# Two mixture layers after a dynamic convolution on one core: matmuls of 64 rows in both row halves of the array

## Chip, core and metric

The kernel runs on one core of a Trainium2 chip. The metric is the device time of one execution in microseconds; three runs of the kernel before took 1215.25 to 1215.58 us, with a median of 1215.5 us.

## What is computed

A softmax over 7 taps weights a causal convolution of x (2 x 4096 tokens, 192 channels in 8 heads). The result, 8192 tokens of 192 channels, goes through two layers, each a product to 2048 channels, an activation, and a product back to 192:

```python
x = attn_out.reshape(B * S, D)                       # 8192 x 192
h = x @ w_in; g = where(h >= 1, h, where(h <= -1, 0, (h + 1) ** 2 / 4)); x = g @ w_out
h = x @ w_in2; g = h - tanh(h);                                          out = g @ w_out2
```

Each product is made from a high and a low part of both operands, so that its precision is near that of float32: high x high, low x high and high x low. Low x low isn't needed.

## The kernel before

The tokens are cut into 16 blocks `b` of 512. A **stream** `(m, b)` is layer `m` (0 or 1) on block `b`; from block 3 on the streams alternate, (0, b) and then (1, b - 1). A stream has 16 **items** `(m, b, f)`, one for every 128 of the 2048 channels. An item is:

- the first product, `mm1` (L626 to L630): five matmuls of 128 rows x 128 columns with 512 tokens streamed, into one of the PSUM banks 6, 7, 0, 1. The 192 channels of x are one tile of 128 rows for high (`xt[:, 0]`), one for low (`xt[:, 1]`), and one that holds the other 64 channels, high in its upper 64 rows and low in the lower 64 (`xt[:, 2]`). The weights of the last 64 channels stand twice, once per 64 rows. So the fifth matmul, low weights x `xt[:, 2]`, spends 64 of its rows on low x low.
- the activation: for layer 0 on ScalarE twice (L636, L637) and VectorE (L638), for layer 1 on ScalarE (L640) and VectorE (L641); then the high part `gh` on ScalarE (L642) and the low part `gl` on VectorE (L646).
- the second product, `mm2a` and `mm2b` (L654 to L656, L660, L661): five matmuls onto two banks per stream (2 and 3 for layer 0, 4 and 5 for layer 1), which are added up over the 16 items. It comes three items later (`LAG`).

`finish1` (L682 on) turns the two banks of layer 0 into the next layer's x; `finish2` (L701 on) stores those of layer 1. `conv` makes the convolution of a block on VectorE; from block 4 on (`MOVED`) its result is transposed by VectorE in squares of 32 and by way of HBM (`move_rows`, the buffers `spot`), and not on TensorE.

The order of the work on each engine is fixed by a planner, `Plan.run`: each task has a key (the item's number in the order of items, plus an offset), a duration, what it depends on and which buffers it takes, and each engine starts the ready task with the lowest key. VectorE fills its gaps with the convolution of later blocks as far as buffers allow. Within an engine the instructions then run in that order; semaphores order them between engines. Matmuls have no semaphores among themselves, since TensorE runs them one after the other. GpSimd works only in the first items (up to item 56).

Of the kernel before, what the change touches and what calls it, by code (L numbers as in the profile page):

```python
# [157 lines left out]
def on(engine, dur):  # L158
    return {engine: (dur, 0.0)}
# [3 lines left out]
def tile_dynconv_moe_moe(  # L163
# [71 lines left out]
    def bits(w):  # L235
# [119 lines left out]


    xdone = {}
    a_of, b_of = {}, {}

    def conv(b, banks, base, gap):  # L360
        early = b < EARLY
# [186 lines left out]
    def move_rows(b, wg, xw, mem, xt, dep, key):  # L548


        Q = P // 32
        hi_sb = prod_sb.bitcast(F32R)

        area = lambda n: xws[xw.n].rearrange("p j d -> p (j d)")[:, n * T * D:(n + 1) * T * D]

        def squares(e, n, src):
            e.transpose(
                area(n).rearrange("p (c j n) -> p j c n", c=D // 32, j=T),
                src.rearrange("p j (c n) -> p j c n", n=32),
            )  # L560
# [8 lines left out]
        spot = slot("spot")  # L569

        def away(e, n):
            if n == 0:
                spots[spot.n] = dram.tile([2, D, N], F32, tag=f"spot{spot.n}", name=f"spot{b}")
            for q in range(Q):
                to = spots[spot.n][n].rearrange("(c k) t -> k c t", k=32)[:, :, q * P:(q + 1) * P]
                e.dma_start(to, area(n)[q * 32:(q + 1) * 32].rearrange("p (c k) -> p c k", c=D // 32))

        def back(e, n, k):
            if n == 0 and k == 0:
                xt_tile(xt, f"a_{b}")  # L580
            xt_, d = xt_t[xt.n].bitcast(F32), spots[spot.n][n]
            if k == 0:
                e.dma_start(xt_[:, n, :], d[0:P])
            else:
                e.dma_start(xt_[n * D1:(n + 1) * D1, 2, :], d[P:D])

        d0 = plan.add(on("DMA", 2.6), last, lambda e: away(e, 0), [tq], takes=[spot], uses=[xw], late=4.0)
        d1 = plan.add(on("DMA", 2.6), last, lambda e: away(e, 1), [tr, d0], uses=[xw, spot], late=4.0)
        moves = []
        for n, k in ((0, 0), (0, 1), (1, 0), (1, 1)):  # L590
            first = [] if moves else [marks["fin1", b - 1]]
            moves.append(plan.add(
                on("DMA", 1.0), last, lambda e, n=n, k=k: back(e, n, k), [d1 if n else d0] + moves[:1] + first,
                takes=[] if moves else [xt], uses=[spot] + ([xt] if moves else []), late=3.0,
            ))
        xdone[0, b] = moves

# [14 lines left out]
        return (2, 3) if b == 0 else (4, 5)  # L612

    prev1, prev2 = [None], {}

    def item(m, b, f, after):
        i = at[m, b, f]
# [7 lines left out]

        def mm1(e):  # L626
            w, xt = win[m], xt_t[xs.n]
            ops = [(0, 0), (2, 0), (0, 1), (1, 2), (3, 2)]
            for n, (k, c) in enumerate(ops):
                e.matmul(ps[h.n], w[:, k, fs], xt[:, c], start=n == 0, stop=n == len(ops) - 1)  # L630

        first = plan.add(on("PE", 1.135), i, mm1, after + xdone[m, b] + [wdone.get((0, m, f // 2))], takes=[h], uses=[xs], late=0.35)
# [15 lines left out]
        w = wout[m][:, f, :]  # L648
        a, z = f == 0, f == NF - 1
        need = [wdone.get((1, m, f // 2)), prev2.get((m, b))]  # L650
        if m == 0 or b < NB - 1:
# [12 lines left out]
            t = plan.add(on("PE", 0.454), i + LAG + 0.5, mm2b, [t, tlo], uses=[gl] + acc, late=0.35)  # L664
        else:
            def mm2(e):
                q = banks()
                for n in range(T):
                    ts = slice(n * P, (n + 1) * P)
                    if not z:  # L670
                        e.matmul(q[n][:, 0:2 * D], GH()[:, ts], w, start=a, stop=False)  # L671
                    e.matmul(q[n][:, P:P + D], GL()[:, ts], w[:, P:P + D], start=False, stop=False)
                    if z:
                        e.matmul(q[n][:, 0:2 * D], GH()[:, ts], w, start=False, stop=True)

            t = plan.add(on("PE", 1.14), i + LAG + 0.5, mm2, [thi, tlo] + need, takes=acc if a else [], uses=[gh, gl] + ([] if a else acc), late=0.35)
# [5 lines left out]
    def finish1(b, acc, key, t):  # L682
        s, tm = slot("xt"), slot("val")
        b_of[b] = s
        X, M = lambda k: xt_t[s.n][:, k], lambda: vals[tm.n][0:D1]
        p0, p1 = lambda: ps[acc[0].n], lambda: ps[acc[1].n]

        def hi(e):
            xt_tile(s, f"b_{b}")
            e.copy(X(0), p0())  # L690

        h0 = plan.add(on("ACT", 0.60), key, hi, [t], takes=[s], uses=acc)
        h1 = plan.add(on("ACT", 0.60), key, lambda e: e.copy(M(), p1()[D1:P]), [t], takes=[tm], uses=acc)
# [5 lines left out]
        xdone[1, b] = [h0, l0, rh, rl]  # L699

    def finish2(b, acc, key, t):  # L701

        s, tm = slot("raw"), slot("val")
        R = lambda: raws[s.n].rearrange("p a b -> p (a b)").bitcast(F32)
        M = lambda: vals[tm.n][0:D1]
        p0, p1 = lambda: ps[acc[0].n], lambda: ps[acc[1].n]
# [14 lines left out]
            plan.add(on("DMA", 2.6), key, lambda e, c=c: store(e, c), [t0 if c < P // 32 else t1], uses=[s], late=3.0)  # L721

    def finish_last(b, acc, key, t):
        s = slot("raw")
# [21 lines left out]
    for m in range(2):  # L746
        for c in range(NF // 2):
            for kind in range(2):
                weights(kind, m, c, LEAD[m])
    after = {}  # L750
# [60 lines left out]
```

## Time and profile before

| | |
|---|---|
| median of 3 runs | 1215.5 us (1215.25 to 1215.58) |
| the profiled execution, its span | 1214.0 us; its own time beyond the span isn't listed apart |
| TensorE busy | 1177.7 us, 97%, 5192 matmuls |
| TensorE weight loads busy | 967.7 us, 80%, beside the matmuls |
| VectorE busy | 995.7 us, 82% |
| ScalarE busy | 838.7 us, 69% |
| GpSimd busy | 98.7 us, 8%, all in the first 200 us |
| DMA | 58.4 MB, mean 48 GB/s |

The busy time of an engine is the union of its instructions' spans. A matmul's record, 0.39 us here, is longer than the distance to the next matmul, since matmuls overlap. The profile calls the engines PE (TensorE; PEld are its weight loads, LDWEIGHTS), DVE (VectorE), ACT (ScalarE), POOL (GpSimd) and SP (the queue that issues DMAs).

### The profile page before, as it was taken

To read this page: it belongs to the slowest core of one execution; us is meant where nothing else is said; L and a number is where in the kernel's file an instruction comes from. 1 tells how busy PE (TensorE), PEld (TensorE's weight loads), DVE (VectorE), ACT (ScalarE), POOL (GpSimd) and SP (SyncE) were. 2 spreads that over 40 slices of the span, in tenths; PEclk is the share of its full clock that TensorE was granted. 3 is DMA by queue.
4 is the path that set the end of the run, shared out by engine and by line. 5 is a ranking of instruction groups with operands and counts; after the bars stand their busy time and mean duration, and the time that the engine had idled before them with its cause. 6 is when DMAs were issued, how large, how long until landed. Compare 5 with 4: busy or idle time off the path is not lost.

```text
span 1214.0 us, 15286 instructions
## 1 busy us (share of the span) xinstructions
PE 1177.7 (97%) x5192; PEld 967.7 (80%) x5192; DVE 995.7 (82%) x1519; ACT 838.7 (69%) x1499; POOL 98.7 (8%) x85
## 2 busy tenths in 40 slices
PE   3899999999999999999999999999999999999998
PEld 2678778888887888888888888888888888888887
DVE  8999998999999999797987969688666666666665
ACT  4989896775757667586675857667576665757653
POOL 4643650000000000000000000000000000000000
PEclk9999999999999999999999999999999999999999
DMA  7422130231231203030030302102020100100000
GB/s 209 148 69 77 52 117 10 53 103 50 72 89 18 60 30 101 1 73 29 11 92 1 102 1 45 54 5 61 1 66 1 19 22 2 39 1 14 1 8 19
DMA packets 92038, 58.40 MB, mean 48 GB/s; under 512 B 55868, under 2 KB 81082, under 8 KB 91960
## 3 DMA queue, kind: packets, MB, share of 16 engines
q1 hardware_dynamic: 91772, 57.05, 17.2%
q8 instruction: 40, 0.66, 0.2%
q10 hardware_dynamic: 188, 0.39, 0.1%
q14 instruction: 38, 0.31, 0.1%
HBM read 41.67 MB, written 15.73 MB: 47 GB/s over the span
## 4 chain that ended last, share of the span: by engine, by line
PE 88%; DVE 5%; ACT 3%; issue 1%; POOL 1%; DMA 1%; SPq 0%; DVEq 0%; ACTq 0%; POOLq 0%
PE ps L630 44%; PE ps L660 9%; PE ps L661 9%; PE ps L654 9%; PE ps L656 8%; PE ps L655 8%; PE ps L671 1%; DVE prod L426 1%; DVE gl L646 1%; DVE g L638 1%; ACT gh L642 1%; ACT g L636 1%; ACT raw L312 0%; DMA wg<-in_weight_gen_dram 0%; DVE acc L473 0%
## 5 line engine op out<-in xcount | busy, mean ns | idle before, releaser
L642 ACT CAST gh<-g 128x512 fp32r<-128x512 f32 x512 | 315.4, 618 | 215.2 <-DVE g L641 175.0
L646 DVE TENSOR_TENSOR gl<-g,gh 128x512 fp32r<-128x512 f32 x474 | 326.8, 692 | 150.9 <-ACT gh L642 148.7
L630 PE MATMUL ps<-a,win 128*128 128x512 f32 x1280 | 335.7, 393 | 5.9 <-POOL win L341 2.8
L630 PE MATMUL ps<-b,win 128*128 128x512 f32 x1280 | 332.4, 390 | 2.3 <-DVE val L321 2.3
L630 PEld LDWEIGHTS ps<-a,win 128*128 128x128 f32 x1280 | 241.6, 189 | 61.6 <-POOL win L341 4.0
L630 PEld LDWEIGHTS ps<-b,win 128*128 128x128 f32 x1280 | 239.1, 188 | 52.5 <-DVE val L321 3.5
L641 DVE TENSOR_TENSOR g<-ps,g 128x512 f32<-128x512 f32 x256 | 175.2, 686 | 28.8 <-ACT g L640 28.7
L660 PE MATMUL ps<-gl,wout 128*128 128x512 f32 x496 | 194.6, 392 | 1.9 <-DVE gl L646 1.3
L654 PE MATMUL ps<-gh,wout 128*128 128x512 f32 x496 | 194.1, 391 | 2.1 <-ACT gh L642 2.0
L636 ACT ACTIVATE g<-ps 128x512 f32<-128x512 f32 x256 | 152.0, 594 | 63.3 <-PE ps L630 57.2
L661 PE MATMUL ps<-gl,wout 128*128 128x512 f32 x496 | 193.5, 390 | 0.0
L655 PE MATMUL ps<-gh,wout 128*128 128x512 f32 x496 | 193.3, 390 | 0.0
L656 PE MATMUL ps<-gh,wout 128*128 128x512 f32 x496 | 193.2, 390 | 0.0
L640 ACT ACTIVATE g<-ps 128x512 f32<-128x512 f32 x256 | 152.1, 596 | 46.4 <-PE ps L630 45.3
L638 DVE SCALAR_TENSOR_TENSOR g<-ps,g 128x512 f32<-128x512 f32 x256 | 173.1, 680 | 10.6 <-ACT g L637 9.5
L637 ACT ACTIVATE g<-g 128x512 f32<-128x512 f32 x256 | 162.1, 633 | 4.0
L660 PEld LDWEIGHTS ps<-gl,wout 128*128 128x128 f32 x496 | 93.3, 188 | 25.4 <-DVE gl L646 4.5
L654 PEld LDWEIGHTS ps<-gh,wout 128*128 128x128 f32 x496 | 93.2, 188 | 23.6 <-ACT gh L642 4.4
L656 PEld LDWEIGHTS ps<-gh,wout 128*128 128x128 f32 x496 | 93.3, 188 | 19.5
L655 PEld LDWEIGHTS ps<-gh,wout 128*128 128x128 f32 x496 | 93.2, 188 | 19.1
L661 PEld LDWEIGHTS ps<-gl,wout 128*128 128x128 f32 x496 | 93.4, 188 | 18.9
L426 DVE TENSOR_TENSOR prod<-xw,wg 128x768 f32<-128x768 f32 x84 | 82.7, 985 | 0.1
(78 smaller groups left out, 594.6 us busy)
## 6 DMA issues: line engine op xcount, KB each, us to landing
xw<-in_x_dram SPq DMA_DIRECT2D x14, 960.0 KB, 4.8
spot<-xw SPq DMA_DIRECT2D x96, 96.0 KB, 2.4
raw<-in_moe_w_out_dram SPq DMA_DIRECT2D x16, 384.0 KB, 3.2
a<-spot SPq DMA_DIRECT2D x24, 256.0 KB, 3.9
out_dram<-raw SPq DMA_DIRECT2D x360, 16.0 KB, 1.5
raw<-in_moe_w_in_dram SPq DMA_DIRECT2D x16, 256.0 KB, 3.1
raw<-in_moe_w_in_dram SPq DMA_DIRECT2D x32, 128.0 KB, 3.3
a<-spot SPq DMA_DIRECT2D x24, 128.0 KB, 3.7
```

The costliest lines, as they stand in the source:

```text
L630: e.matmul(ps[h.n], w[:, k, fs], xt[:, c], start=n == 0, stop=n == len(ops) - 1)
L636: t = plan.add(on("ACT", 0.60), i, lambda e: e.activation(G_(), H_(), AF.Relu, bias=0.5, scale=0.5), [first], takes=[g], uses=[h], late=0.1)
L637: t = plan.add(on("ACT", 0.537), i, lambda e: e.activation(G_(), G_(), AF.Square), [t], uses=[g])
L638: t = plan.add(on("DVE", 0.605), i, lambda e: e.scalar_tensor_tensor(G_(), H_(), 1.0, G_(), op0=ALU.max, op1=ALU.min), [t], uses=[g, h])
L641: t = plan.add(on("DVE", 0.605), i, lambda e: e.tensor_tensor(G_(), H_(), G_(), op=ALU.subtract), [t], uses=[g, h])
L642: thi = plan.add(on("ACT", 0.527), i, lambda e: e.copy(GH(), G_()), [t], takes=[gh], uses=[g])
L646: tlo = plan.add(engines, i, lambda e: e.tensor_tensor(GL(), G_(), GH().bitcast(F32), op=ALU.subtract), [thi], takes=[gl], uses=[g], lock= ...
L654: e.matmul(p0, w[:, P:2 * P], GH(), start=a, stop=False)
L655: e.matmul(p0, w[:, 0:P], GH(), start=False, stop=False)
L656: e.matmul(p1, w[:, 2 * P:], GH(), start=a, stop=False)
L660: e.matmul(p1, w[:, 2 * P:], GL(), start=False, stop=z)
L661: e.matmul(p0, w[:, P:2 * P], GL(), start=False, stop=z)
```

## The change

In 24 of the 32 streams, (0, 4) to (0, 15) and (1, 3) to (1, 14), no matmul has 128 rows. Each is made by halves, one on rows 0 to 63 of the array (lane 0) and one on rows 64 to 127 (lane 1), with the matching rows of weights and tokens. The fifth matmul of the first product needs one half alone. Two items are taken together (`both`): 18 halves of first products and 20 of second products, issued as 19 steps with one half of each lane (`weave`).

The two lanes are never on the same bank at once. Steps 0 to 8 (`one`): lane 0 has the first products of both items, while lane 1 has its half of the second products of two earlier items. Steps 9 to 13 (`two`) and 14 to 18 (`three`): lane 0 has its half of two second products and lane 1 its half of the two first products. Where a lane takes a bank over, its matmul waits for the other lane's last matmul on it: `relay` puts an empty instruction on GpSimd that waits for that matmul, and `behind` makes the later matmul wait for the relay. The marks are `a`, `b`, `p` and `q`; `b` goes from lane 1's matmul of step 9 to lane 0's of step 12, `p` from lane 0's of step 16 to lane 1's of step 0 of the next block, that is step 19.

For the halves of the fifth matmul in lane 1, the high part of the last 64 channels is needed in rows 64 to 127 too: a tile `x3` in the place of raw buffers 2 and 3, filled by one more DMA per block of layer 0 and one more ScalarE copy per block of layer 1, 12 each. `finish2` stages its output in the raw buffers 0 and 1 alone. After (1, 14) `close` runs the last ten halves of lane 1 by themselves, and (1, 15) runs as before.

```diff
+    def paired(m, b):
+        return b >= MOVED - m and (m, b) != (1, NB - 1)
...
+    HALVES = [slice(0, D1), slice(D1, P)]
...
+    def relay(q):
+        r = nc.gpsimd.nop(nofuse=True)
+        tc.add_manual_dep(r.ins, q.ins.name, SYNC)
+        return r
+
+    def behind(q, r):
+        if r is not None:
+            tc.add_manual_dep(q.ins, r.ins.name, SYNC)
...
+    def chunks(lane, m, b, f, h, xs):
+        rs, fs = HALVES[lane], slice(f * P, (f + 1) * P)
+        ops = [(0, 0), (2, 0), (0, 1), (1, 2)] + ([(3, 2 + lane)] if f % 2 == lane else [])
+        def mm(e, n, k, c):
+            x = x3(x3_of[m, b]) if c == 3 else xt_t[xs.n][rs, c]
+            return e.matmul(ps[h.n], win[m][rs, k, fs], x, start=lane == 0 and n == 0, stop=lane == 1 and n == len(ops) - 1)
...
+    def weave(e, low, high, waits, marks_at):
+        for n in range(max(len(low), len(high))):
+            for lane, ops in ((0, low), (1, high)):
+                if n < len(ops):
+                    q = ops[n](e)
+                    behind(q, fence.get(waits.get((lane, n))))
+                    if (lane, n) in marks_at:
+                        fence[marks_at[lane, n]] = relay(q)
...
+    def both(m, b, f, h0, h1, need):
+        i = at[m, b, f]
+        g0, g1, o0, o1 = i - 3, i - 2, i - 5, i - 4
...
+        def one(e):
+            low = chunks(0, m, b, f, h0, xs) + chunks(0, m, b, f + 1, h1, xs)
+            high = (old_p() + old_q())[:9]
+            weave(e, low, high, {(1, 0): "p", (1, 6): "q"}, {(1, 5): "a"} if have else {(0, 5): "a", (0, 8): "b"})
+        def two(e):
+            low = second(0, 0, g0, P_KINDS) + second(0, 1, g0, Q_KINDS)
+            high = old_q()[3:] + chunks(1, m, b, f, h0, xs)
+            n = len(high) - 4
+            weave(e, low, high, {(0, 0): "a", (0, 3): "b", (1, n): "a"}, {(1, 0): "b"} if n else {})
+        def three(e):
+            low = second(0, 0, g1, P_KINDS) + second(0, 1, g1, Q_KINDS)
+            high = chunks(1, m, b, f + 1, h1, xs)
+            weave(e, low, high, {(1, 0): "b"}, {(0, 2): "p", (0, 4): "q"})
...
+        if paired(1, b):
+            s3 = x3_of[1, b] = slot("x3")
+            xdone[1, b].append(plan.add(on("ACT", 0.525), key, lambda e: e.copy(x3(s3), M()), [r] + x3_free, takes=[s3], uses=[tm]))
...
-        s, tm = slot("raw"), slot("val")
+        s, tm = slot("raw", out_raws), slot("val")
...
+            if (m, b, f) == (1, NB - 2, NF - 1):
+                close(at[m, b, f] + 1)
```

How the change orders TensorE's work: before, in a stream of layer 0, an item's first product (`win0`, into a bank such as `ps7`) is followed by the second product of the item three before it (`wout0`, onto banks 2 and 3, which are one tile `ps2`); `x5` are five matmuls in a row.

```order
L630 MATMUL ps7_68<-a_9_4924,win0_81 128x512 x5
L654 MATMUL ps2_63<-gh0_98,wout0_83 128x512 [waits Activation_49]
L655 MATMUL ps2_63<-gh0_98,wout0_83 128x512
L656 MATMUL ps2_63<-gh0_98,wout0_83 128x512
L660 MATMUL ps2_63<-gl2_104,wout0_83 128x512 [waits DVE_49]
L661 MATMUL ps2_63<-gl2_104,wout0_83 128x512
L630 MATMUL ps0_65<-a_9_4924,win0_81 128x512 x5
```

In the change, on TensorE at the start of `two` in such a stream, each row is one half; L669 are halves of second products and L685 of first products. The first two rows are the two halves of step 9.

```order
L669 MATMUL ps2_63<-gh1_99,wout0_83 128x512 [waits Pool_sequencer_49,Activation_49]
L669 MATMUL ps2_63<-gl3_105,wout0_83 128x512
L669 MATMUL ps2_63<-gh1_99,wout0_83 128x512
L685 MATMUL ps6_67<-a_9_6614,win0_81 128x512
L669 MATMUL ps2_63<-gl1_103,wout0_83 128x512 [waits DVE_49]
L685 MATMUL ps6_67<-a_9_6614,win0_81 128x512
L669 MATMUL ps2_63<-gh1_99,wout0_83 128x512 [waits Pool_sequencer_49]
L685 MATMUL ps6_67<-a_9_6614,win0_81 128x512
```

The halves now alternate, and the second row's completion, passed on through GpSimd's sequencer (`b`), is what the seventh row waits for, three steps later. The row at step 9 waits for two semaphores.

At the end of `three`, on TensorE too, the last rows before the next block's step 0 are these:

```order
L669 MATMUL ps2_63<-gl2_104,wout0_83 128x512 [waits DVE_49]
L685 MATMUL ps7_68<-a_9_6614,win0_81 128x512
L669 MATMUL ps2_63<-gh0_98,wout0_83 128x512
L685 MATMUL ps7_68<-a_9_6614,win0_81 128x512
L669 MATMUL ps2_63<-gl2_104,wout0_83 128x512
L685 MATMUL ps7_68<-x3_3_3014,win0_81 128x512
L685 MATMUL ps0_65<-a_9_6614,win0_81 128x512
L669 MATMUL ps2_63<-gh1_99,wout0_83 128x512 [waits Pool_sequencer_49]
```

The first row is step 16, which waits for `gl` of the first item of the block before, and its completion is the mark `p`; the last row, lane 1 in step 0 of the next block, waits for that.

## Rows read from the trace of the kernel before

**Rows 1.** The page's part 1: busy us (share of the span) xinstructions of each engine.

```profile
span 1214.0 us, 15286 instructions
PE 1177.7 (97%) x5192; PEld 967.7 (80%) x5192; DVE 995.7 (82%) x1519; ACT 838.7 (69%) x1499; POOL 98.7 (8%) x85
```

**Rows 2.** The page's part 4: the chain that ended last, by line.

```profile
PE ps L630 44%; PE ps L660 9%; PE ps L661 9%; PE ps L654 9%; PE ps L656 8%; PE ps L655 8%; PE ps L671 1%; DVE prod L426 1%; DVE gl L646 1%; DVE g L638 1%; ACT gh L642 1%; ACT g L636 1%; ACT raw L312 0%; DMA wg<-in_weight_gen_dram 0%; DVE acc L473 0%
```

**Rows 3.** Waits of TensorE, 270 to 1168 us: us in total, times, longest.

```profile
PE ps L660 <- DVE gl L646: 0.5, 1, 0.5
```

**Rows 4.** Timeline, 700 to 706 us: start us, us, engine, line, operation.

```profile
700.68 0.39 PE L661 MATMUL ps<-gl,wout 128*128 128x512 f32 x1
700.68 1.09 PEld L630 LDWEIGHTS ps<-b,win 128*128 128x128 f32 x5
700.91 1.30 PE L630 MATMUL ps<-b,win 128*128 128x512 f32 x5
...
702.30 0.60 ACT L640 ACTIVATE g<-ps 128x512 f32<-128x512 f32 x1 [0.29 <-PE ps L630]
...
702.93 0.69 DVE L641 TENSOR_TENSOR g<-ps,g 128x512 f32<-128x512 f32 x1 [0.20 <-ACT g L640]
...
703.86 0.63 ACT L642 CAST gh<-g 128x512 fp32r<-128x512 f32 x1
...
704.60 0.68 DVE L646 TENSOR_TENSOR gl<-g,gh 128x512 fp32r<-128x512 f32 x1
```

**Rows 5.** The same place of a later item, TensorE's timeline from 1168 us.

```profile
1169.88 0.39 PE L661 MATMUL ps<-gl,wout 128*128 128x512 f32 x1
```

**Rows 6.** Weight loads of the last two transposes, and the next, timeline from 203 us.

```profile
203.98 0.25 PEld L514 LDWEIGHTS ps<-ident,xw 128*128 128x128 f32 x2
...
204.20 0.53 PEld L630 LDWEIGHTS ps<-b,win 128*128 128x128 f32 x3
```

**Rows 7.** Timeline, 57 to 66 us: who starts after whom.

```profile
57.78 1.13 ACT L642 CAST gh<-g 128x512 fp32r<-128x512 f32 x2
...
58.52 1.61 POOL L646 TENSOR_TENSOR gl<-g,gh 128x512 fp32r<-128x512 f32 x1 [3.33 <-ACT gh L642]
...
59.37 1.31 DVE L646 TENSOR_TENSOR gl<-g,gh 128x512 fp32r<-128x512 f32 x1
...
60.73 0.19 PEld L660 LDWEIGHTS ps<-gl,wout 128*128 128x128 f32 x1 [0.89 <-DVE gl L646]
...
60.84 0.19 PEld L661 LDWEIGHTS ps<-gl,wout 128*128 128x128 f32 x1
...
64.05 0.39 PE L656 MATMUL ps<-gh,wout 128*128 128x512 f32 x1
...
64.47 0.62 ACT L642 CAST gh<-g 128x512 fp32r<-128x512 f32 x1 [0.36 <-PE ps L656]
```

**Rows 8.** Line L511: an instruction of TensorE's queue alone; ns min/median/max.

```profile
L511 PEldq EVENT_SEMAPHORE  x3: 51/51/51, 17.9 to 203.5; - x3
```

**Rows 9.** Windows of 296 to 470 and 850 to 1168 us: length, busy of each engine, clock.

```profile
core 0: us, PE busy (x) PEld busy (x) DVE busy (x) ACT busy (x) POOL busy (x), PEclk, DMA share, GB/s
296.00:470.00 174.00, 173.28 (x759) 141.38 (x758) 171.13 (x266) 119.50 (x214) 0.00 (x0) 1.00 0.20 53
850.00:1168.00 318.00, 318.00 (x1404) 263.31 (x1404) 204.43 (x308) 209.47 (x363) 0.00 (x0) 1.00 0.07 16
```

**Rows 10.** Timeline, 336 to 346 us: one item through the vector engines, and a DMA issue.

```profile
336.43 1.30 PE L630 MATMUL ps<-b,win 128*128 128x512 f32 x5
...
338.81 0.45 SPq L585 DMA_DIRECT2D a<-spot  x1
...
339.68 0.59 ACT L640 ACTIVATE g<-ps 128x512 f32<-128x512 f32 x1
...
341.37 0.63 ACT L642 CAST gh<-g 128x512 fp32r<-128x512 f32 x1
...
342.57 0.66 DVE L646 TENSOR_TENSOR gl<-g,gh 128x512 fp32r<-128x512 f32 x1
```

More of the change, by code (lines that the diff above doesn't have):

```diff
@@ L226, in tile_dynconv_moe_moe, with x3 @@
     xt_t = {}
+    x3_t = {}
+    def x3(s):
+        n, k = divmod(s.n, 2)
+        if n not in x3_t:
+            x3_t[n] = const.tile([P, 2, N], F32R, tag=f"raw{n}", name=f"x3_{n}")
+        return x3_t[n][D1:P, k]
     def xt_tile(s, name, shape=(P, 3, N), dt=F32R):
@@ L244, in tile_dynconv_moe_moe @@
         "g": [0, 1, 2], "gh": list(range(LAG + 1)), "gl": list(range(LAG + 1)), "bank": list(range(8)), "spot": [0, 1],
+        "x3": [4, 5, 6, 7],
     }
@@ L357, in tile_dynconv_moe_moe @@
     xdone = {}
-    a_of, b_of = {}, {}
+    a_of, b_of, x3_of = {}, {}, {}
+    x3_free = []
     def conv(b, banks, base, gap):
@@ L569, in move_rows @@
         spot = slot("spot")
+        xs3 = x3_of[0, b] = slot("x3")
         def away(e, n):
@@ L585, in back @@
                 e.dma_start(xt_[n * D1:(n + 1) * D1, 2, :], d[P:D])
+            if (n, k) == (0, 1):
+                e.dma_start(x3(xs3).bitcast(F32), d[P:D])
         d0 = plan.add(on("DMA", 2.6), last, lambda e: away(e, 0), [tq], takes=[spot], uses=[xw], late=4.0)
@@ L592, in move_rows @@
             moves.append(plan.add(
-                on("DMA", 1.0), last, lambda e, n=n, k=k: back(e, n, k), [d1 if n else d0] + moves[:1] + first,
-                takes=[] if moves else [xt], uses=[spot] + ([xt] if moves else []), late=3.0,
+                on("DMA", 1.0), last, lambda e, n=n, k=k: back(e, n, k), [d1 if n else d0] + moves[:1] + first + (x3_free if len(moves) == 1 else []),
+                takes=[xs3] if len(moves) == 1 else [] if moves else [xt], uses=[spot] + ([xt] if moves else []), late=3.0,
             ))
@@ L614, in tile_dynconv_moe_moe, with lanes1, lanes2 @@
     prev1, prev2 = [None], {}
+    partner = {}
+    def paired(m, b):
+        return b >= MOVED - m and (m, b) != (1, NB - 1)
+    def lanes1(i):
+        return i < len(order) and paired(*order[i][:2])
+    def lanes2(i):
+        return lanes1(i + 3 - (i + 3) % 2)
+    HALVES = [slice(0, D1), slice(D1, P)]
+    SYNC = mybir.DependencyInfo(mybir.DependencyClass.Sync, mybir.DependencyReason.DATA)
+    late2 = {}
+    last = [None]
+    fence = {}
+    def relay(q):
+        r = nc.gpsimd.nop(nofuse=True)
+        tc.add_manual_dep(r.ins, q.ins.name, SYNC)
+        return r
@@ new lines, in behind, with second, mm @@
+    def behind(q, r):
+        if r is not None:
+            tc.add_manual_dep(q.ins, r.ins.name, SYNC)
+    def second(lane, which, g, kinds):
+        if g not in late2:
+            return []
+        m, b, f, w, gh, gl, GH, GL, acc, need = late2[g]
+        rs, to = HALVES[lane], lambda: ps[acc[which].n]
+        out = []
+        for c, low in kinds:
+            def mm(e, c=c, low=low, n=len(out)):
+                return e.matmul(
+                    to(), w[rs, c:c + P], (GL() if low else GH())[rs],
+                    start=f == 0 and lane == 0 and n == 0, stop=f == NF - 1 and lane == 1 and n == len(kinds) - 1,
+                )
+            out.append(mm)
+        return out
@@ new lines, in tile_dynconv_moe_moe @@
+    P_KINDS, Q_KINDS = [(P, False), (0, False), (P, True)], [(2 * P, False), (2 * P, True)]
+    def chunks(lane, m, b, f, h, xs):
[4 more added lines that the diff above has]
+            return e.matmul(ps[h.n], win[m][rs, k, fs], x, start=lane == 0 and n == 0, stop=lane == 1 and n == len(ops) - 1)
+        return [lambda e, n=n, k=k, c=c: mm(e, n, k, c) for n, (k, c) in enumerate(ops)]
@@ new lines, in weave, with used @@
+    def weave(e, low, high, waits, marks_at):
[6 more added lines that the diff above has]
+                        fence[marks_at[lane, n]] = relay(q)
+    def used(*gs):
+        out = []
+        for g in gs:
+            if g in late2:
+                out += [late2[g][4], late2[g][5]] + late2[g][8]
+        return out
@@ new lines, in done @@
+    def done(g, t):
+        if g in late2 and late2[g][2] == NF - 1:
+            m, b, f, *_, acc, need = late2[g]
+            (finish1 if m == 0 else finish2)(b, acc, g + 7.0, t)
+    def both(m, b, f, h0, h1, need):
+        i = at[m, b, f]
+        xs = a_of[b] if m == 0 else b_of[b]
+        g0, g1, o0, o1 = i - 3, i - 2, i - 5, i - 4
+        old_p = lambda: second(1, 0, o0, P_KINDS) + second(1, 0, o1, P_KINDS)
+        old_q = lambda: second(1, 1, o0, Q_KINDS) + second(1, 1, o1, Q_KINDS)
+        have = o0 in late2
+        def one(e):
[11 more added lines that the diff above has]
+            weave(e, low, high, {(1, 0): "b"}, {(0, 2): "p", (0, 4): "q"})
+        opens = [s for g in (g0, g1) if late2[g][2] == 0 for s in late2[g][8]]
+        rest = lambda g: [s for s in used(g) if s not in opens]
+        t = plan.add(on("PE", 2.08), i, one, need + [last[0]], takes=[h0, h1], uses=[xs, x3_of[m, b]] + used(o0, o1), late=0.0)
+        done(o0, t)
+        mid = plan.add(on("PE", 1.155), i, two, [t] + late2[g0][9], takes=[s for s in opens if s in late2[g0][8]], uses=[h0, xs] + used(o1) + rest(g0), late=0.35)
+        done(o1, mid)
+        end = last[0] = plan.add(on("PE", 1.155), i + 1, three, [mid] + late2[g1][9], takes=[s for s in opens if s in late2[g1][8]], uses=[h1, xs, x3_of[m, b]] + rest(g1), late=0.35)
+        prev2[late2[g1][:2]] = end
+        return mid, end
@@ L616, in item, with close, one @@
+    def close(i):
+        o0, o1 = i - 5, i - 4
+        def one(e):
+            high = [mm for w, k in ((0, P_KINDS), (1, Q_KINDS)) for o in (o0, o1) for mm in second(1, w, o, k)]
+            weave(e, [], high, {(1, 0): "p", (1, 6): "q"}, {})
+        t = plan.add(on("PE", 2.3), i, one, [last[0]], uses=used(o0, o1), late=0.35)
+        done(o0, t)
+        done(o1, t)
+        prev2[late2[o1][:2]] = t
     def item(m, b, f, after):
@@ L627, in mm1 @@
             w, xt = win[m], xt_t[xs.n]
[L628 to L632, printed above, removed]
+            for n, (k, c) in enumerate([(0, 0), (2, 0), (0, 1), (1, 2), (3, 2)]):
+                e.matmul(ps[h.n], w[:, k, fs], xt[:, c], start=n == 0, stop=n == 4)
+        need1 = after + xdone[m, b] + [wdone.get((0, m, f // 2))]
+        if not lanes1(i):
+            first = plan.add(on("PE", 1.135), i, mm1, need1, takes=[h], uses=[xs], late=0.35)
+        elif f % 2 == 0:
+            h1 = slot("bank", h_banks(m, b))
+            first, second = both(m, b, f, h, h1, need1)
+            partner[m, b] = h1, second
+        else:
+            h, first = partner[m, b]
         marks["mm1", m, b, f] = first
@@ L650, in item @@
         need = [wdone.get((1, m, f // 2)), prev2.get((m, b))]
+        if lanes2(i):
+            late2[i] = m, b, f, w, gh, gl, GH, GL, acc, [thi, tlo] + need
+            return first
         if m == 0 or b < NB - 1:
@@ L699, in finish1, with out_raws @@
         xdone[1, b] = [h0, l0, rh, rl]
+        if paired(1, b):
+            s3 = x3_of[1, b] = slot("x3")
+            xdone[1, b].append(plan.add(on("ACT", 0.525), key, lambda e: e.copy(x3(s3), M()), [r] + x3_free, takes=[s3], uses=[tm]))
+    def out_raws():
+        return (0, 1)
     def finish2(b, acc, key, t):
-        s, tm = slot("raw"), slot("val")
+        s, tm = slot("raw", out_raws), slot("val")
         R = lambda: raws[s.n].rearrange("p a b -> p (a b)").bitcast(F32)
@@ L723, in finish_last @@
     def finish_last(b, acc, key, t):
-        s = slot("raw")
+        s = slot("raw", out_raws)
         O = lambda: raws[s.n].rearrange("p a b -> p (a b)")[:, 0:T * D].bitcast(F32).rearrange("p (t d) -> p t d", t=T)
@@ L749, in tile_dynconv_moe_moe @@
                 weights(kind, m, c, LEAD[m])
+    x3_free += [wdone[kind, 1, c] for kind in range(2) for c in range(NF // 2)]
     after = {}
```

## The prediction

> **What bounds the kernel now.** I read the page's busy line first, then the chain, the waits of TensorE, the timeline, and the windows by stage. The busy line shows TensorE at 97% of the span and the chain has its matmul lines on nearly all of its length [rows 1, 2]. Busy time alone proves little, so the waits decide: between 270 and 1168 us TensorE waited once, for 0.5 us [rows 3]. In the timeline the matmul of L661 at 700.68 us is followed by the five of L630 from 700.91 us; the same place of a later item is at 1169.88 us [rows 4, 5]. 469.20 us are 207 items of ten matmuls, so a matmul costs 0.2267 us and an item 2.267 us, at the full granted clock (1.00 in both windows of [rows 9]). The profiled span is 1214.0 us, and the median 1215.5 us: some 1.5 us lie around it, and the sum below starts at 1215.5.
>
> So the time can only fall if TensorE does less, and that is what the change is about. The fifth matmul of the first product spends half of its rows on a part that isn't needed. In 64-row halves an item is 9 + 10 halves, not 20, and two items are 19 steps of two halves where 20 whole matmuls stood. 24 streams of 16 items are 192 blocks of two items.
>
> **The step.** Nothing in this trace has 64 rows. Below: each half still streams 512 columns, so a step can't be shorter than the whole matmul's 0.2267 us. Above: if the halves took turns, 0.453 us. What could part them is the weight loads, now two per step. The nearest rows are the loads of the transposes, which come 0.11 us apart, each with its matmul: 203.98 to 204.20 us for two [rows 6]. They also bound the issue of instructions, four in 0.22 us. Two loads at 0.11 are 0.22, under 0.2267. I take 0.2267 for an undisturbed step and 0.11 for a load of 64 rows (between nothing and 0.11; the row is of 128 rows and the same 128 columns).
>
> By the Trainium skill, page "TensorE: Matmul & The Clock Gate", section "LDWEIGHTS (loading the stationary operand)", a load takes as long as it has columns, whatever its rows; this speaks against the change, which doubles the loads and makes none cheaper. No run so far shows a load of 64 rows; by the page the 0.11 stands, and with loads at half of it the relays below would cost nothing and the sum would be 11 us lower.
>
> A block then goes from 20 x 0.2267 = 4.534 us to 19 x 0.2267 = 4.307 us, and 192 blocks give at most 43.5 us.
>
> **The relays.** A matmul that takes over a bank now waits until the other half's last matmul on it is done, by way of GpSimd. The tight places are three steps apart: the upper half's matmul of step 9 to the lower half's of step 12, and the lower half's of step 16 to the upper half's of step 19. Behind the waiting load the whole matmul queue stands, both halves. The price of a pass: a matmul's record is 0.39 us [rows 4]; the hop r follows, and then the load. For r, low end: TensorE's end to ScalarE's start 0.03 (64.44 to 64.47), a queue instruction 0.05, VectorE's end to TensorE's load 0.05 (60.68 to 60.73) [rows 7, 8]: 0.13. High end: 0.09 from TensorE to ScalarE (702.21 to 702.30, [rows 4]), 0.17 from ScalarE to a real GpSimd operation (58.34 to 58.52) and 0.05: 0.31. I take 0.13, since a relay is a queue instruction and no operation of GpSimd. From step 9 the waiting load starts 0.39 + 0.13 = 0.52 us later, the other half's load behind it, 0.11 each: 0.74 us until the upper half's matmul of step 12, against 3 steps = 0.68. The upper half can't make the 0.06 us up, as it streams without a gap, so every block is 0.06 longer: **4.367 us**. With loads at half or less it is nothing; with r = 0.31 both tight places bind, and the loop of 13 steps and two passes of 0.39 + 0.31 + 0.11 is 2.947 + 1.62 = 4.567 us. The load exposed after a wait costs just 0.11 before the next one starts, 60.73 to 60.84 [rows 7]. GpSimd has no other work in this stage [rows 9], so no relay queues there.
>
> Gain of the blocks: 192 x (4.534 - 4.367) = **32.1 us** (between 43.5 and -6.3).
>
> **The halves that stay alone.** `close` runs ten upper halves with nothing beside them: 10 x 0.2267 = +2.3 us. Two changes between whole and half rows, at the first pair and before the last stream: at most the tail of a matmul, 0.39 - 0.23, and a load, so +0.6 us for both.
>
> **Later results for the second product.** In a block the first item's last half is at step 13, and its low part `gl` is wanted by a load at step 34 (step 15 of the next block): 21 x 0.2267 - 0.39 = 4.37 us. In a quiet stage the way from the matmuls' end to the end of `gl` takes 702.21 to 705.28 = 3.1 us [rows 4], and the first layer has one more ScalarE operation of some 0.6: it fits. In the stage from 296 to 470 us VectorE is busy 98% [rows 9], with convolution in each gap, and the way there takes 337.73 to 343.23 = 5.5 us [rows 10]; today nobody waits for it. There `gl` would be 1.1 us late. The loop from one late block to the next runs over two blocks, so one pays about half, 0.55 us, if VectorE's order stays as it is. Those 174 us hold some 38 blocks, and the convolutions after them are shorter bursts. Nothing lost is the low end; the high end is 38 x 0.55 = 21 us. I take **+6 us**: the stage keeps about its present pace (38 x 0.167 = 6.3), since VectorE is full there and empties once TensorE waits. From 850 us on VectorE is at 64% and nothing is lost.
>
> **Small edits, costed at nothing.** Twelve copies to `x3` on ScalarE, like the casts of 0.62 [rows 10], lie ahead of a stream that starts one stream later, on an engine at 69% [rows 1]. Twelve more DMAs on SP, an issue of 0.45 us each [rows 10], go out with the transfers back from `spot`, long before they are read. Without that cover each would cost its 0.6 or 0.5 us once, 13 us in all. The output's staging keeps two raw buffers of four, and needs one per stream of the second layer, that is one in some 72 us.
>
> Sum: 1215.5 - 32.1 + 2.3 + 0.6 + 6 = **1192.3 us**.
>
> **The rivals.**
> *Nothing lost.* Loads of 64 rows are cheap, or relays quick, and VectorE's order fits: 1215.5 - 43.5 + 2.9 = 1175. For it: r and the load are both at the margin. Against: VectorE at 98%.
> *The vectors are the next bound.* `gl` is late in all of the dense stage, 21 us and not 6: 1207. For it: 5.5 against 4.37 us. Against: the plan orders VectorE's work anew.
> *Slow relays (slower than before).* The pass is two semaphores and a third queue. From r = 0.29 on (2.947 + 2 x (0.50 + r) = 4.53) a block is no shorter than now; at 0.31, with the other terms, 1215.5 + 6.3 + 8.9 = 1231. For it: the 0.17 us to GpSimd. Against: that row is an operation, not a queue instruction.
> *The halves don't overlap as the change says.* Loads that queue at their full record of 0.19 [rows 7] make a step 0.38 and a block 7.2 us: 1215.5 + 192 x 2.69 = 1730. Against: the loads 0.11 apart.
> The Trainium skill, same page, section "Measured speedup vs the span model", has four row tiles at 3.07 times and not 4. An estimate from that ratio is a step of 0.295 us, and about 1420 us; no run so far bears on it.
>
> **How the numbers follow.** Forecast as summed (1180 to 1204): 0.62. Nothing lost: 0.10. Vectors: 0.08. No change within 0.2%, which is about what a measurement of this kernel can tell: 0.04, the case of r just under 0.29. Slow relays 0.11, halves apart 0.05. Faster is 0.62 + 0.10 + 0.08 = 0.80, slower 0.16. The range leaves out the halves that don't overlap, the slower part of the relays and the very best: 1174 to 1222. The forecast's own range is 1180 to 1204.
>
> **What would show it.** In the timeline after 285 us, two matmuls should start within some 0.1 us, and two of a half 0.227 us apart; blocks of 4.36 us. TensorE's idle time by releaser should name GpSimd's relays for little and `gl` for some microseconds between 290 and 470 us, and almost nothing from 850 us on. The granted clock should stay at 1.00. A step of 0.23 or more everywhere would mean that loads bind; blocks of over 4.5 us with waits on GpSimd, that the relays do.

## The result and the profile after

The changed kernel takes **1200.2 us** (median of 4 runs, 1199.5 to 1201.1), where the kernel before, on the same chip, took 1215.4 us (1215.2 to 1215.6). The ratio is 0.987, with an interval of 0.9856 to 0.9885: 15.2 us faster. The forecast was 1192.0 us and its range 1174 to 1222. The profiled execution took 1199.51 us, its span is 1197.7 us; the span before was 1214.0 us [rows 1].

The page of the kernel after, its part 1 and the head of part 4 (the chain by engine, then by line). L685 are the halves of first products, L669 those of second products, L773 the whole matmuls of first products that are left:

```profile
span 1197.7 us, 23410 instructions
PE 1151.5 (96%) x8648; PEld 1034.3 (86%) x8648; DVE 994.1 (83%) x1519; ACT 849.1 (71%) x1511; POOL 98.6 (8%) x85
...
PE 76%; DVE 14%; issue 4%; ACT 3%; DMA 2%; POOL 0%; SPq 0%; DVEq 0%; ACTq 0%; POOLq 0%
```

TensorE still bounds the kernel, but VectorE now holds 14% of the chain, where it was 5% before. The waits of TensorE from 285 to 1150 us name it (engine, line, what it waited for: us in total, times, longest; first of the matmuls, then of the weight loads, which stand ahead of them):

```profile
PE ps L669 <- DVE gl L797: 7.2, 14, 0.8
PE ps L669 <- ACT gh L793: 0.3, 1, 0.3
```

```profile
PEld ps L669 <- DVE gl L797: 21.6, 32, 1.2
PEld ps L669 <- ACT gh L793: 8.7, 21, 0.7
PEld ps L685 <- issue: 0.4, 1, 0.4
```

Before, the matmuls' list was one wait of 0.5 us [rows 3], and the loads' list, from 285 to 1168 us, was this:

```profile
PEld ps L660 <- DVE gl L646: 2.7, 6, 0.9
PEld ps L654 <- ACT gh L642: 0.7, 2, 0.5
```

GpSimd's relays are in none of the lists. A load can come late while the matmul ahead of it still streams, and then the list of the loads shows more than that of the matmuls: at 597.34 us, below, the load waited 0.75 us and its matmul 0.32 us, and the block is 0.68 us late. The same stage in windows, to be held against [rows 9]:

```profile
core 0: us, PE busy (x) PEld busy (x) DVE busy (x) ACT busy (x) POOL busy (x), PEclk, DMA share, GB/s
...
296.00:470.00 174.00, 170.80 (x1443) 146.56 (x1443) 169.51 (x265) 125.07 (x217) 0.00 (x0) 1.00 0.20 55
470.00:700.00 230.00, 226.52 (x1947) 208.91 (x1945) 194.21 (x299) 160.66 (x281) 0.00 (x0) 1.00 0.19 53
700.00:850.00 150.00, 147.73 (x1272) 136.62 (x1270) 121.16 (x179) 103.53 (x180) 0.00 (x0) 1.00 0.13 36
850.00:1120.00 270.00, 270.00 (x2375) 265.23 (x2374) 180.53 (x274) 192.77 (x333) 0.00 (x0) 1.00 0.08 20
```

TensorE has gaps up to 850 us and none after. The granted clock is 1.00 throughout, so the clock explains nothing here.

**Blocks.** One half per block reads `x3` (shown as `x`), so the distance of two such halves is a block. Two that are 56 blocks apart, in the quiet part, TensorE's timeline:

```profile
876.54 0.39 PE L685 MATMUL ps<-x,win 64*128 64x512 f32 x1
...
1118.83 0.39 PE L685 MATMUL ps<-x,win 64*128 64x512 f32 x1
```

242.29 / 56 = 4.327 us: 19 steps of 0.2267 us, which are 4.307, and 0.020. And a stream of the first layer, block after block:

```profile
588.57 0.39 PE L685 MATMUL ps<-x,win 64*128 64x512 f32 x1
...
592.90 0.39 PE L685 MATMUL ps<-x,win 64*128 64x512 f32 x1
...
597.91 0.39 PE L685 MATMUL ps<-x,win 64*128 64x512 f32 x1
...
602.29 0.39 PE L685 MATMUL ps<-x,win 64*128 64x512 f32 x1
...
606.62 0.39 PE L685 MATMUL ps<-x,win 64*128 64x512 f32 x1
...
611.63 0.39 PE L685 MATMUL ps<-x,win 64*128 64x512 f32 x1
...
617.22 0.40 PE L685 MATMUL ps<-x,win 64*128 64x512 f32 x1
```

The blocks are 4.33, **5.01**, 4.38, 4.33, **5.01** and **5.59** us. Every second stream, that of the first layer, has these three late blocks until 842 us, five such streams after 482 us; the blocks of the second layer's streams there are at 4.33 to 4.36, and all blocks from 842 us on at 4.33. Before 482 us late blocks come irregularly.

What happens in the block from 592.90 to 597.91, timeline of all engines:

```profile
595.13 0.58 ACT L877 COPY val<-ps 64x512 f32<-64x512 f32 x1 [0.17 <-PE ps L669]
595.14 0.95 DVE L484 TENSOR_TENSOR acc<-acc,prod 128x768 f32<-128x768 f32 x1
...
595.62 0.62 ACT L793 CAST gh<-g 128x512 fp32r<-128x512 f32 x1
...
596.01 0.68 DVE L789 SCALAR_TENSOR_TENSOR g<-ps,g 128x512 f32<-128x512 f32 x1
...
596.61 0.68 DVE L797 TENSOR_TENSOR gl<-g,gh 128x512 fp32r<-128x512 f32 x1
...
597.34 0.18 PEld L669 LDWEIGHTS ps<-gl,wout 64*128 64x128 f32 x1 [0.75 <-DVE gl L797]
...
597.34 0.18 PEld L685 LDWEIGHTS ps<-a,win 64*128 64x128 f32 x1
```

On ScalarE `finish2`'s copy (L877) stands ahead of `gh`, and on VectorE a convolution addition (L484) and the next item's activation (L789) stand ahead of `gl`. `gl` ends at 597.29, and 0.05 us later the load for it starts, with the other half's load behind it in the same queue.

**The account of the halves' stage.** TensorE's timeline of the kernel before, where the first item of the 24 streams begins, and the first item after them:

```profile
295.01 0.84 PE L630 MATMUL ps<-a,win 128*128 128x512 f32 x3
...
1167.84 0.62 PE L630 MATMUL ps<-b,win 128*128 128x512 f32 x2
```

That is 872.8 us for 384 items; 384 x 2.267 = 870.4, so 2.4 us were lost there before. After, the stage goes from 294.94 to 1151.70 us, 856.8 us, 16.1 us less (the spans differ by 16.3, the medians by 15.2): 3.80 to the first `x3` half, 191 blocks of 4.327 = 826.5, **23.9 us of lateness** (the mean of the 191 blocks is 4.452), and 2.58 from the last `x3` half on, which holds `close` with ten steps of 0.227. Of the 23.9 us, 10.2 lie before 482 us and 13.7 after.

### The profile page after: what moved, and what is told of

Same layout as the page of the kernel before. It is cut to its first block, busy times and chain, and to the rows that moved or that the text cites. A ratio compares the mean times of both kernels' runs of the same rounds, so it can differ in the third digit from the quotient of the medians.

```text
span 1197.7 us, 23410 instructions
## 1 busy us (share of the span) xinstructions
PE 1151.5 (96%) x8648; PEld 1034.3 (86%) x8648; DVE 994.1 (83%) x1519; ACT 849.1 (71%) x1511; POOL 98.6 (8%) x85
## 4 chain that ended last, share of the span: by engine, by line
PE 76%; DVE 14%; issue 4%; ACT 3%; DMA 2%; POOL 0%; SPq 0%; DVEq 0%; ACTq 0%; POOLq 0%
PE ps L669 33%; PE ps L685 29%; PE ps L773 7%; DVE gl L797 3%; DVE g L789 3%; DVE acc L484 1%; PE ps L814 1%; PE ps L808 1%; DVE prod L437 1%; PE ps L815 1%; PE ps L809 1%; PE ps L810 1%; PE ps L825 1%; DVE g L792 1%; ACT gh L793 1%
## 5 line engine op out<-in xcount | busy, mean ns | idle before, releaser
L669 PE MATMUL ps<-gh,wout 64*128 64x512 f32 x2304 | 730.2, 388 | 0.8 <-ACT gh L793 0.3
L669 PE MATMUL ps<-gl,wout 64*128 64x512 f32 x1536 | 597.2, 390 | 8.2 <-DVE gl L797 7.2
L669 PEld LDWEIGHTS ps<-gh,wout 64*128 64x128 f32 x2304 | 417.9, 184 | 29.2 <-ACT gh L793 8.7
L685 PE MATMUL ps<-a,win 64*128 64x512 f32 x1632 | 413.6, 391 | 0.0
L685 PE MATMUL ps<-b,win 64*128 64x512 f32 x1632 | 403.4, 387 | 0.0
L669 PEld LDWEIGHTS ps<-gl,wout 64*128 64x128 f32 x1536 | 282.9, 184 | 26.8 <-DVE gl L797 21.6
L685 PEld LDWEIGHTS ps<-a,win 64*128 64x128 f32 x1632 | 296.5, 184 | 8.3 <-issue 0.4
L685 PEld LDWEIGHTS ps<-b,win 64*128 64x128 f32 x1632 | 299.9, 184 | 3.8
L789 DVE SCALAR_TENSOR_TENSOR g<-ps,g 128x512 f32<-128x512 f32 x256 | 173.1, 682 | 51.0 <-ACT g L788 50.7
L773 PE MATMUL ps<-a,win 128*128 128x512 f32 x320 | 85.8, 402 | 7.6 <-POOL win L351 2.7
L773 PE MATMUL ps<-b,win 128*128 128x512 f32 x320 | 83.7, 392 | 2.3 <-DVE val L331 2.3
L773 PEld LDWEIGHTS ps<-a,win 128*128 128x128 f32 x320 | 60.6, 192 | 25.2 <-POOL win L351 4.0
L685 PE MATMUL ps<-x,win 64*128 64x512 f32 x192 | 74.4, 387 | 0.0
L773 PEld LDWEIGHTS ps<-b,win 128*128 128x128 f32 x320 | 58.8, 188 | 15.4 <-DVE val L331 3.6
L484 DVE TENSOR_TENSOR acc<-acc,prod 128x768 f32<-128x768 f32 x70 | 68.2, 974 | 0.1
```

The costliest lines, as they stand in the source:

```text
L484: e.tensor_tensor(prods[k % 2] if early and k == mine - 1 else acc_sb, acc_sb, prods[k % 2], op=ALU.add)
L669: return e.matmul(to(), w[rs, c:c + P], (GL() if low else GH())[rs], start=f == 0 and lane == 0 and n == 0, stop=f == NF - 1 and lane == 1 ...
L685: return e.matmul(ps[h.n], win[m][rs, k, fs], x, start=lane == 0 and n == 0, stop=lane == 1 and n == len(ops) - 1)
L789: t = plan.add(on("DVE", 0.605), i, lambda e: e.scalar_tensor_tensor(G_(), H_(), 1.0, G_(), op0=ALU.max, op1=ALU.min), [t], uses=[g, h])
```

## The experiments

Three theories stood at the start. **A**: `gl` and `gh` come late because VectorE and ScalarE have convolution and `finish2` work ahead of them, so room in time (a later second product, or a convolution spread out) cures it. **B**: `gh` and `gl` wait for a free buffer, since the halves hold the buffers of an item longer. From 296 to 860 us VectorE waits 10.9 us in 34 cases for a second product before a `gl`, and ScalarE 17.7 us in 37 cases before a `gh`, which speaks for B. **C**: the relays cost the time.

**e1, second products one block later**, with two more buffers each for `gh` and `gl`, for which `x3` gets a tile of its own and `xt` four buffers instead of five:

```diff
-        g0, g1, o0, o1 = i - 3, i - 2, i - 5, i - 4
+        g0, g1, o0, o1 = i - 5, i - 4, i - 7, i - 6
...
-        "g": [0, 1, 2], "gh": list(range(LAG + 1)), "gl": list(range(LAG + 1)), "bank": list(range(8)), "spot": [0, 1],
+        "g": [0, 1, 2], "gh": list(range(LAG + 3)), "gl": list(range(LAG + 3)), "bank": list(range(8)), "spot": [0, 1],
```

> The changed kernel, with the second products taken one block (two items) later, two more gh and two more gl buffers, and four x buffers instead of five to pay for them. Theory A (gl and gh come too late because the first item of a block has only some 4.4 us for its way through ScalarE and VectorE; 27 of 192 blocks lose 24 us in sum): the way gets 8.7 us, nearly all blocks run at 4.33 us, and the time is 1174 to 1182 us. Theory B (four gh and gl buffers hold ScalarE and VectorE up until the upper half has used them): the same time as the run with more buffers alone. Theory C (the relays cost the 24 us): no change from 1200 us.

Measured: 1186.4 us, ratio 0.9761 [0.9745, 0.9777]. From 410 us on every block but the last, of 5.89, is 4.33 us, so the room in time does what A says. But one block takes 11.45 us, which is why the sum falls short (timeline of the three engines):

```profile
372.94 0.96 DVE L444 TENSOR_TENSOR prod<-xw,wg 128x768 f32<-128x768 f32 x1
373.01 0.39 PE L692 MATMUL ps<-x,win 64*128 64x512 f32 x1
...
376.39 0.96 DVE L580 TENSOR_TENSOR acc<-acc,prod 128x768 f32<-128x768 f32 x1
...
377.27 1.28 DVE L796 SCALAR_TENSOR_TENSOR g<-ps,g 128x512 f32<-128x512 f32 x2
377.38 0.83 ACT L581 CAST prod<-acc 128x768 fp32r<-128x768 f32 x1 [5.90 <-DVE acc L580]
...
378.01 0.79 PE L692 MATMUL ps<-a,win 64*128 64x512 f32 x1 [4.61 <-DVE g L796]
```

ScalarE stood 5.9 us in its queue at a convolution's cast, and on VectorE an activation that frees a PSUM bank (L796) stood behind a run of convolution. TensorE waited 4.6 us. A later second product doesn't help a first product that has no bank.

**e2, the buffers alone** (e1's buffers, the old distance) and **e4, the control** (four `xt` instead of five, nothing else):

> The changed kernel with two more gh and two more gl buffers and four x buffers instead of five, and no more lag. Theory A: within 1195 to 1204 us, since the allowance of the first item is the same. Theory B: ScalarE's 17.7 us and VectorE's 10.9 us of waits for the upper halves go, and the time falls to 1178 to 1186 us. Theory C: 1200 us.

> The changed kernel with four x buffers instead of five and nothing else, the control for the two runs with more buffers. Theory A: convolutions run less far ahead but in the same bursts, 1195 to 1204 us. Theories B and C: 1200 us.

Measured: e2 1199.0 us, 0.9864 [0.9849, 0.9879]; e4 1199.7 us, 0.987 [0.9855, 0.9884]. Neither can be told from the change itself. In e2 the waits of VectorE and ScalarE for second products are gone from both lists, and TensorE's loads still wait 28.4 us for `gl` and `gh` from 296 to 860 us (30.3 in the change). So B falls, and the room taken from `xt` costs nothing.

**e3, the convolution spread out.** From block 4 on, each VectorE operation of a convolution also waits for the first product of an item, one about 1.6 items further on with each operation, beginning 56 items ahead of its stream:

```diff
+        def gate():
+            n = at[0, b, 0] - AHEAD + int(PACE * count[0])
+            return [marks["mm1", *order[n]]] if b >= MOVED else []
...
-                on("DVE", 0.87), key(), fn, dep + [whole(k), lh], takes=([] if kind or k else [mem] + (area2 if b == 0 else [])),
+                on("DVE", 0.87), key(), fn, dep + [whole(k), lh] + gate(), takes=([] if kind or k else [mem] + (area2 if b == 0 else [])),
```

> The changed kernel, in which each VectorE operation of a convolution from block 4 on waits for the first product of an item, one operation per 1.6 items, from 56 items ahead of its stream. Theory A (the convolutions that fill VectorE in bursts make gl late): at most one such operation meets an item's way, most of the late blocks go, 1180 to 1190 us. Theory B: the buffers are as short as before, 1195 to 1202 us. Theory C: 1200 us.

Measured: 1178.0 us, 0.9689 [0.9675, 0.9704], 22 us below the change and somewhat below the 1180 to 1190 expected. TensorE's matmuls have no wait at all from 285 to 1160 us and its loads 2.2 us for `gl`, no block is over 4.7 us, and the mean is 4.336. The windows, as above:

```profile
296.00:470.00 174.00, 174.00 (x1521) 167.87 (x1521) 149.72 (x228) 128.48 (x224) 0.00 (x0) 1.00 0.18 46
470.00:700.00 230.00, 230.00 (x2018) 220.90 (x2016) 200.50 (x307) 165.10 (x287) 0.00 (x0) 1.00 0.19 51
850.00:1120.00 270.00, 270.00 (x2373) 263.05 (x2371) 213.82 (x320) 195.08 (x338) 0.00 (x0) 1.00 0.13 30
```

The work of VectorE has gone from the first window to the last (169.51 to 149.72 us, and 180.53 to 213.82). From 470 to 700 us it even does more than in the change, 200.50 against 194.21 us, and nobody waits: what made `gl` late there was the order, not the amount. A is confirmed, and C falls, since e3 has the same relays.

**e7, the same spreading on the kernel before**, and **e8, e1 and e3 together**:

> The kernel before with the same spread convolutions. Theory A: it has 7 us for the same way and TensorE never waits for VectorE there, so nothing changes: 1213 to 1217 us. Rival, spreading is worth 20 us to any of these kernels: 1190 to 1200 us.

> Both remedies, a block more of lag with two more gh and gl buffers, and spread convolutions. Theory A: each alone removes the late blocks, so together they add little: all blocks at 4.33 us, 1174 to 1179 us. If something else than late results is left in the spread run's blocks of 4.35 to 4.41, no change from 1178 us.

Measured: e7 1213.9 us, 0.9978 [0.9969, 0.9987]; e8 1178.8 us, 0.9691 [0.9676, 0.9705]. Without the halves the spreading is worth 0.2%, about the 2.4 us that the kernel before lost in this stage: all but that of its 22 us is lateness that the halves made. Once the convolution is spread, the later second product adds nothing: the late blocks that e3 still has are gone, but 186 blocks of e8 are 4.333 us instead of 4.327, and the last is 5.90. Why is open.

**e6, twenty steps.** On e3, both halves of the fifth matmul again, low x low included as before the change; the pass `b` has four steps from mark to load instead of three:

```diff
-        ops = [(0, 0), (2, 0), (0, 1), (1, 2)] + ([(3, 2 + lane)] if f % 2 == lane else [])
+        ops = [(0, 0), (2, 0), (0, 1), (1, 2), (3, 2)]
```

> The run with spread convolutions, with the fifth half matmul of the first product in both halves for each item, that is low x low again, so 20 steps for two items. Theory (the only gain is the step that falls away): blocks of 20 x 0.2267 + 0.02 = 4.55 us, some 43 us more, 1219 to 1224 us, no better than the kernel before. Rival, matmuls of half the rows gain by themselves: under 1205 us.

Measured: 1216.7 us, 1.0002 [0.9992, 1.0011]. That is below the 1219 to 1224 expected: a block is 4.533 us (the same half of a second product starts at 903.34 and 907.87 us), which is 20 steps of 0.2267 without the 0.020. It stands 38.7 us above e3 (on another chip; some 38 by the ratios), 0.20 us per block: a step of 0.227, less the 0.02 that the passes cost in 19 steps. Against e7, whole matmuls with the same spreading, it is 2.8 us longer, of which `close` and the changes of mode were 2.1 in the change. So in their own stage halves by themselves gain nothing and lose nothing against whole matmuls; the whole gain is the twentieth step.

**e5, slow relays.** On e3, the relay is a real GpSimd operation:

```diff
-        r = nc.gpsimd.nop(nofuse=True)
+        r = nc.gpsimd.memset(slow_t, 0.0)
```

> The run with spread convolutions, in which each relay is a small GpSimd memset of a buffer of its own instead of an empty instruction. In the changed kernel a relay's hop r, from the end of the record of a matmul to the start of the load that waits, reads 0.105 us; with an operation I expect 0.25 to 0.30 us. Theory of the loop (13 steps and two passes of 0.39 + r + 0.11): with r = 0.27 a block takes 2.95 + 1.54 = 4.49 us instead of 4.33, and the time rises by some 31 us to 1205 to 1213 us. Rival, the relays have room to spare: 1177 to 1181 us and blocks of 4.33.

Measured: 1226.6 us, 1.0084 [1.0069, 1.0099], slower than before and well above the 1205 to 1213 expected. All blocks but one are 4.567 us, and the loads' list from 285 to 1160 us names the relay; then a pass, in the timeline:

```profile
PEld ps L676 <- POOL slow L659: 47.2, 188, 0.3
```

```profile
904.47 0.39 PE L676 MATMUL ps<-gl,wout 64*128 64x512 f32 x1
...
904.98 0.10 POOL L659 MEMSET slow<- 128x8 f32 x1 [1.61 <-PE ps L676]
905.14 0.18 PEld L676 LDWEIGHTS ps<-gh,wout 64*128 64x128 f32 x1
```

The mark ends at 904.86, the load starts at 905.14: r = 0.28. The prediction's loop gives 2.947 + 2 x (0.39 + 0.28 + 0.11) = 4.507 us. Of the 0.06 us more, 0.05 lie in the steps between the passes: lane 1's steps 1 to 9 start at 905.47 and 907.32 us and lane 0's steps 13 to 16 at 908.34 and 909.03, so these eleven take 2.54 us and not 2.49. Why they run at 0.231 us is open, as it is after the pass in the change.

**e9, more steps between.** On e3, lane 0's steps 9 to 18 in another order: after `g0`'s three halves on the first bank come two of `g1` on it, then the rest, then the second bank. So the pass `b` has six steps and `p` five, but `gl` is wanted two steps earlier:

```diff
-            low = second(0, 0, g0, P_KINDS) + second(0, 1, g0, Q_KINDS)
+            low = second(0, 0, g0, P_KINDS) + second(0, 0, g1, P_KINDS)[:2]
...
-            low = second(0, 0, g1, P_KINDS) + second(0, 1, g1, Q_KINDS)
+            low = second(0, 0, g1, P_KINDS)[2:] + second(0, 1, g0, Q_KINDS) + second(0, 1, g1, Q_KINDS)
```

> The run with spread convolutions, with the lower half's steps 9 to 18 in another order: both items' matmuls for the first bank, then those for the second. The pass b then has six steps instead of three and the pass p five instead of three. Theory (the 0.02 us by which a block is longer than 19 steps come from the three steps of pass b, after which four steps read 0.230 to 0.233 us): all steps 0.227, blocks of 4.307 us, 3.8 us less, 1173 to 1176 us, unless gl, now wanted two steps earlier, comes late. Rival, the 0.02 us belong to something else: 1178 us.

Measured: 1192.6 us, 0.98 [0.9784, 0.9817]. 101 of the 191 blocks are 4.307 us, exactly 19 steps: the 0.020 us is gone, so it belonged to the passes. But 46 blocks are 4.54 to 4.95 us, and the loads' waits say why:

```profile
PEld ps L675 <- DVE gl L803: 22.3, 45, 0.6
PEld ps L675 <- ACT gh L799: 6.3, 22, 0.3
```

**e10, all three**: e9's order, e1's later second product, e3's spreading.

> The same order with a block more of lag and two more gh and gl buffers. Theory: blocks of 4.307 us with no late ones, 1172 to 1176 us. Rival: 1178 us.

Measured: **1174.3 us**, 0.9654 [0.9639, 0.9668], the fastest version. Two `x3` halves 56 blocks apart:

```profile
851.21 0.39 PE L698 MATMUL ps<-x,win 64*128 64x512 f32 x1
...
1092.38 0.39 PE L698 MATMUL ps<-x,win 64*128 64x512 f32 x1
```

241.17 / 56 = 4.307 us, 187 of 191 blocks: as short as 19 steps can be. Here the later second product, worthless in e8, pays for the two steps that the order takes from `gl`.

**e11, e9 with e5's slow relay**:

> The same order, with a GpSimd memset as each relay. Theory of the passes: with a hop of 0.28 us a pass takes 0.39 + 0.28 + 0.11 = 0.78 us or 3.4 steps, and the shortest now has four: blocks of 4.307 us and the time of the run in this order with empty relays, within 2 us. Rival, each relay costs time on TensorE's queue wherever it stands: 1215 to 1225 us, as with slow relays in the old order.

Measured: 1207.7 us, 0.9925 [0.9911, 0.994]. A quiet block is 4.40 us, against 4.567 in the old order. More steps between the marks forgive most of a slow relay, not all: the run was expected within 2 us of e9, and is 15 us above it. The 0.09 us left don't sit at one pass. The loads' list from 285 to 1160 us names no relay, and steps away from the marks are longer too, here lane 0's steps 9 and 17:

```profile
905.81 0.39 PE L676 MATMUL ps<-gh,wout 64*128 64x512 f32 x1
...
907.66 0.39 PE L676 MATMUL ps<-gh,wout 64*128 64x512 f32 x1
```

Eight steps in 1.85 us are 0.231 each. Whether the pass `a`, which the order leaves at four steps, sets this off isn't shown.

## Why the prediction was right in sign and 8 us too low

- **The step, right.** An undisturbed step is 0.2267 us, so the two halves do run beside one another, and the rival of halves apart falls, and with it the estimate of 0.295 us from the four row tiles of the Trainium skill, page "TensorE: Matmul & The Clock Gate", section "Measured speedup vs the span model": two halves cost what one whole matmul cost, and twenty such steps in e6 what twenty whole matmuls did (no run here has four tiles).
- **The loads, wrong in a way that helped.** The prediction let the two halves' loads take turns at 0.11 us each. They don't, as the next fence shows: they start at 905.25 and 905.26 and run beside one another. So the second load, half of what made the relays dear in the sum, costs nothing. The record of a load is 0.184 us with 64 rows and 0.188 with 128; this agrees with the Trainium skill, page "TensorE: Matmul & The Clock Gate", section "LDWEIGHTS (loading the stationary operand)", by which rows don't count.
- **The relays, 3.8 us where 11.5 were forecast.** The hop was 0.13 us in the sum and is 0.10. The pass `b` in the kernel after (TensorE's timeline, and the relay on GpSimd's queue: ns min/median/max, first and last start):

```profile
904.76 0.39 PE L669 MATMUL ps<-gl,wout 64*128 64x512 f32 x1
...
905.22 0.39 PE L685 MATMUL ps<-a,win 64*128 64x512 f32 x1
905.25 0.18 PEld L669 LDWEIGHTS ps<-gh,wout 64*128 64x128 f32 x1
905.26 0.18 PEld L685 LDWEIGHTS ps<-a,win 64*128 64x128 f32 x1
905.37 0.39 PE L669 MATMUL ps<-gh,wout 64*128 64x512 f32 x1
...
906.07 0.39 PE L669 MATMUL ps<-gh,wout 64*128 64x512 f32 x1
```

```profile
L652 POOLq EVENT_SEMAPHORE  x1: 17/17/17, 905.2 to 905.2; - x1
```

  The mark, step 9, ends at 905.15; the relay takes 17 ns; the waiting load starts at 905.25 and its matmul at 905.37, 0.61 us after the mark's start, where three steps are 0.68: lane 0 is in time, lane 1 too. What is left is that the next steps run at 0.233 us (905.37 to 906.07 is three), which makes the 0.020 us; e9 and e10 show that it goes with the tight pass. 192 x 0.020 = 3.8.
- **Slow relays, a rival that the chip could have had.** From r = 0.29 on, the prediction said, the change gains nothing. e5 has 0.28 and loses 0.8%. The loop was the right one and a little too kind. Its high end of 0.31 rests on a misreading: the row of casts at 57.78 us [rows 7] is two casts, the first is 0.608 us long and ends at 58.39, not 58.34, so it is 0.13 us to GpSimd's operation and 0.27 in all. The empty instruction, and not the GpSimd engine, made the difference: 0.10 against 0.28.
- **`close` and the change of modes, right**: 2.9 were forecast, and 3.80 + 2.58 us around the `x3` halves, less one block of 4.31, are 2.1.
- **The later results, the step that failed.** "I take +6 us" should have been 24, or 21.5 against the 2.4 that the kernel before lost in the same stage. In the dense stage 6 was a fair size (10.2, inside the 0 to 21). The error is the half sentence that left out what comes after: "the convolutions after them are shorter bursts". 13.7 us lie there. The allowance of 4.37 us binds one item at a time, so the mean load of VectorE, 84% from 470 to 700 us, says nothing of it: a burst of convolution operations of 0.95 us, put ahead of `gl` by the planner, makes three blocks in a stream late by 0.68, 0.68 and 1.26 us; in the block shown `finish2`'s copy ahead of `gh` has its part in it. That nothing is lost from 850 us on was right.
- **The small edits, right.** No wait on `x3` or its copies shows in either list.

Term by term in the stage: -43.5 (steps) + 3.8 (relays) + 23.9 (late) + 2.1 (ends) - 2.4 (lost before already) = -16.1 us. That the time lies within the forecast's own 1180 to 1204 is in part luck: the late results cost 15.5 us more than the sum has, and the relays 7.7 and the ends 0.8 less.

## What to carry to other kernels

When a change shortens the time between an engine's result and its use, compare the new allowance with the longest way that any single item takes, burst by burst, and not with the busy share of a stage. A slack that a tight order spends must be bought elsewhere: here spreading the background work gave back 22 us, and a longer distance between producer and consumer let a better order have its last 4. And a hand-over between two engines is cheap, though not free, as long as the steps between are longer than record, hop and load together: 0.02 us a block in the change and 0.09 in e11. Count that sum before counting instructions.

## What was not expected of the hardware

- The weight loads of the two row halves start within 0.01 us of each other (905.25 and 905.26) and run side by side; loads for whole rows came 0.11 us apart [rows 6].
- A semaphore passed on by GpSimd's queue costs 0.10 us from TensorE's end to TensorE's load with an empty instruction of 17 ns, and 0.28 us with a small memset whose own record is 0.10.
- In e1, after the 4.6 us without a matmul, the granted clock was half (1.2 GHz of the two levels) and the steps 0.43 us until some 383 us, so the wait cost more than its length; its block is 7.1 us longer than the others:

```profile
378.00:382.00 4.00, 3.99 (x18) 3.17 (x20) 4.00 (x7) 3.50 (x7) 0.00 (x0) 0.50 0.69 238
```
